# Attention in an MLP kernel: one float32 product, a reciprocal root from the table, later stages, batches hosted elsewhere

## The chip, the core and the metric

The kernel runs on one core of a Trainium2 chip. The metric is the device time of one execution in microseconds (us). The engines are named as the profile names them: PE is TensorE (PEld its weight loads), DVE is VectorE, ACT is ScalarE, POOL is GpSimd, SP is SyncE, which only issues DMAs here.

## The reference

Linear attention on 8 batches of 8 heads, 576 rows and 64 columns, then a normalisation by the root of the mean square, then two MLPs (512 to 2048 to 512) on the 4608 rows:

```python
kv  = np.einsum('bhsd,bhse->bhde', k, v)
out = np.einsum('bhsd,bhde->bhse', q, kv)
rms = np.sqrt(np.mean(out * out, axis=-1, keepdims=True) + 1e-06)
x   = out / rms * g_norm                      # then (b, s, h*e): 4608 x 512

h = x @ w_in                                  # first MLP
g = np.where(h >= 1, h, np.where(h <= -1, 0.0, (h + 1) ** 2 / 4))
x = g @ w_out
h = x @ w_in2                                 # second MLP
x = np.maximum(h, 0) ** 2 @ w_out2
```

## The kernel before

**Products.** The large products are made of three passes in a reduced-precision float32 format: an operand is split into a high part (a CAST on ACT, line 221) and the rest (a subtraction on DVE), and `mm3` (line 242) sums high by high, low by high and high by low. A tile of 128 x 512 in this format is one matmul.

**Order of the MLP work.** Five plain blocks come first: block b is the first MLP of batch b, 32 slots of 12 matmuls of 128x512 (4 output tiles of `ph` or 4 accumulators `acc`, three passes each). In a block, `u` is the activation's chain from `ph` (ACT lines 704 and 228, DVE line 706), and `gs` its split, which the `acc` matmuls read. Then six pairs of batches go through products with fewer multiplications (sums of blocks of the matrices, as in Strassen's method): `in_phase` makes `ph` at line 880, `out_phase` makes `po` at line 880, 336 matmuls each. The first two pairs are the second MLP of batches 0 to 3, the next two the first MLP of batches 5 and 6 with 7, and what follows is the second MLP of the rest.

**Attention.** It comes in pieces of two heads, (b, hp), four for each batch. `load_kv`, `load_q` fetch k, v, q through SP's queue. `kv_stage` makes `pkv` = k'v on PE (line 486) and copies its two diagonal blocks into `kvbd` as a high part (ACT, line 221) and a low part (DVE, line 499). `t_stage` transposes q on DVE and splits it (ACT line 221, DVE line 567). `o_stage` makes half of `po` by `mm3`, and from it two squares on ACT (lines 588, 589) and a scaled copy `o`. `r_stage` splits the squares (line 594), sums them over a head on PE (`pr`, line 608: against a matrix of ones, high part and rest), takes ln on ACT (line 609), then exp(-x/2) (line 611) to get a first root `y`, then a square and a Newton step on DVE (lines 526, 622, 623), and hands the result to the MLP as `x` or to DRAM. Two pieces, those in `WHOLE`, have an unsplit float32 product instead (line 576), and batch 0, at the very start, has its own functions (`t_first`, `o_first`, `r_first`). `pkv`, the attention's `po` and `pr` share a pool of two PSUM buffers; `kvbd` has two buffers.

**Where it stands.** `attention(base, every, order)` gives each step a slot. Batches 1 to 4 run in block b - 1, seven slots apart. `HOSTED` places the rest in the first two pairs: six pieces in pair 0 (batch 5, and two of batch 6) and six in pair 1, six slots apart. Block 4 hosts no attention.

**Weight sums.** The pairs need sums of blocks of the weights. They are made during blocks 1 to 4 in 16 units (`units`), 4, 4, 3 and 5 in a block: two loads of 512 KB by SP, some twenty operations of DVE (two are narrowing passes of two operations, two joins, eight sums, six splits), eight of ACT, and six stores of 512 KB that ACT's queue issues. Every engine takes its instructions in the order in which they were written down, so a step that waits holds up what stands behind it on its engine.

Of the kernel before, what the change touches and what calls it, by code (L numbers as in the profile page):

```python
# [10 lines left out]
F32 = mybir.dt.float32  # L11
# [5 lines left out]

LN_SCALE = 2.0**-44  # L20
# [57 lines left out]
def linear_attention_rms_two_mlps(  # L78
# [57 lines left out]
        0: ((5, 0), (5, 1), (5, 2), (5, 3), (6, 0), (6, 2)),  # L136
        1: ((6, 1), (6, 3), (7, 0), (7, 1), (7, 2), (7, 3)),
# [56 lines left out]
    lnb = const.tile([P, 1], F32, name="lnb")  # L194
    expb = const.tile([P, 1], F32, name="expb")
# [3 lines left out]
    kvbd = [const.tile([P, 2, P], F32R, name=f"kvbd{i}") for i in range(2)]  # L199
# [274 lines left out]
    def kv_stage(*pairs):  # L474
# [12 lines left out]
        for n, (b, hp) in enumerate(pairs):  # L487
            for j in range(2):
# [45 lines left out]
    def r_first(hp):  # L534
# [3 lines left out]
        for half in range(2):  # L538
# [3 lines left out]
            nc.scalar.activation(y[:, half], m, AF.Ln, bias=lnb, scale=LN_SCALE)  # L542
# [13 lines left out]
    def t_stage(b, hp):  # L556
        work = [ap1.tile([P, S], F32, tag=f"wk{n}", name=f"wk{n}_{b}_{hp}") for n in range(2)]
        if (b, hp) in WHOLE:
            qT = ap1.tile([P, S], F32, tag="hl0", name=f"qT_{b}_{hp}")
            nc.vector.transpose(qT, qs.pop((b, hp)))  # L560
            hl[b, hp] = (work, qT)
            return
# [33 lines left out]
    def r_stage(b, hp):  # L596
# [18 lines left out]
        for c, m in ms:  # L615
            newton(t[:, c], m)
# [35 lines left out]
    def attention(base, every, order):  # L652

        slots = []
        for j, (b, hp) in enumerate(order):
# [15 lines left out]
            if j == 0 and b < PLAIN:  # L671
                slots.append((s + 6, begin, b))
# [657 lines left out]
```

## Time and profile before

| | |
|---|---|
| device time, median of 3 runs | 1578.36 us (1578.21 to 1580.17) |
| the profiled execution's own time | 1577.18 us |
| its span | 1575.4 us |
| PE busy | 1544.0 us, 98% |
| DVE busy | 1195.8 us, 76% |
| ACT busy | 929.3 us, 59% |
| DMA, mean | 246 GB/s |

The profile is of one execution. A row of a timeline gives a start, a length and in brackets how long the engine had stood still before it and what ended that wait; matmuls overlap, so a row of several matmuls ends with the tail of the last one, and the distance between starts is shorter than a single length. A granted clock of 1.00 is 2.4 GHz; the lower of the two levels is 1.2 GHz.

### The profile page before, as it was taken

Reading aid. Unit: us, or ns where it says so; the run is one execution under the profiler, and the core shown is the slowest. Engines: PE = TensorE matmul, PEld = TensorE weight load, DVE = VectorE, ACT = ScalarE, POOL = GpSimd, SP = SyncE. Lnnn points to the kernel's source line nnn. Section 1 sums busy time; section 2 is a strip of 40 time slices with the busy share of each in tenths; the row PEclk is TensorE's granted clock in tenths of the full one; section 3 lists DMA queues with packets and bytes.
Section 4 is the critical chain, followed back from the end, with each engine's and each line's share of the span. In section 5 each row is a group of like instructions: output and inputs, shape, how many; then the busy total and the mean of one; then the engine's idle time right before and its main releaser. Section 6 shows DMA issues by size and latency. Waiting matters only on the chain.

```text
span 1575.4 us, 22379 instructions
## 1 busy us (share of the span) xinstructions
PE 1544.0 (98%) x7633; PEld 1268.9 (81%) x7633; DVE 1195.8 (76%) x2112; ACT 929.3 (59%) x1751; POOL 13.4 (1%) x30
## 2 busy tenths in 40 slices
PE   9999989999999999999989999999999999999999
PEld 5787768878877788787778888888888888888899
DVE  6975878786989678975689788868974597559666
ACT  5976666766756566735576466546653464446354
POOL 0000000000000000000000000000000000000000
PEclk9999999999999999999999999999999999999999
DMA  9676899796899966878767877776776676977797
GB/s 286 199 246 193 286 307 327 229 292 208 256 353 346 320 195 207 261 219 226 229 199 234 226 242 242 225 220 196 243 232 208 198 243 199 243 236 221 224 387 254
DMA packets 330914, 388.17 MB, mean 246 GB/s; under 512 B 197808, under 2 KB 223408, under 8 KB 330800
## 3 DMA queue, kind: packets, MB, share of 16 engines
q1 hardware_dynamic: 299904, 330.63, 69.2%
q10 hardware_dynamic: 30896, 56.11, 9.5%
q8 instruction: 61, 1.00, 0.3%
q14 instruction: 53, 0.43, 0.1%
HBM read 300.42 MB, written 86.25 MB: 245 GB/s over the span
## 4 chain that ended last, share of the span: by engine, by line
PE 84%; DVE 6%; ACT 5%; DMA 3%; issue 1%; SPq 0%; ACTq 0%; DVEq 0%
PE ph L880 32%; PE po L880 29%; PE acc L242 10%; PE ph L242 9%; PE pkv L486 1%; PE po L242 1%; PE pr L608 1%; DMA wsd<-s 1%; DVE s L189 1%; DVE u L706 1%; PE pwarm L1183 1%; DMA ws<-wsd 1%; DMA rest<-in_v_dram 0%; DVE t L809 0%; DMA wt<-wsd 0%
## 5 line engine op out<-in xcount | busy, mean ns | idle before, releaser
L880 PE MATMUL ph<-x,ws 128*128 128x512 f32 (+1 forms) x2352 | 507.1, 376 | 0.5 <-DVE e L936 0.5
L880 PEld LDWEIGHTS ph<-x,ws 128*128 128x128 f32 x2352 | 419.4, 189 | 79.5 <-DVE e L936 1.2
L880 PE MATMUL po<-t,ws 128*128 128x512 f32 x2016 | 461.7, 390 | 1.5 <-DMA ws<-wsd 0.8
L880 PEld LDWEIGHTS po<-t,ws 128*128 128x128 f32 x2016 | 377.1, 188 | 82.0 <-DVE t L809 3.3
L809 DVE TENSOR_TENSOR t<-g,t 128x512 fp32r<-128x512 f32 (+1 forms) x336 | 215.6, 647 | 84.1 <-ACT t L221 81.7
L221 ACT CAST t<-g 128x512 fp32r<-128x512 f32 (+1 forms) x336 | 195.5, 591 | 120.7 <-PE po L880 62.9
L242 PE MATMUL ph<-x,w 128*128 128x512 f32 x960 | 243.1, 396 | 7.6 <-DVE u L706 6.0
L242 PEld LDWEIGHTS ph<-x,w 128*128 128x128 f32 x960 | 177.4, 189 | 50.5 <-DVE u L706 10.5
L242 PE MATMUL acc<-gs,w 128*128 128x512 f32 x528 | 134.4, 398 | 3.5 <-DVE u L706 1.5
L957 ACT ACTIVATE g<-h 128x512 f32<-128x512 f32 (+1 forms) x120 | 70.4, 589 | 95.8 <-DVE h L946 95.8
L242 PEld LDWEIGHTS acc<-gs,w 128*128 128x128 f32 x528 | 98.6, 190 | 25.6 <-DVE u L706 2.0
L946 DVE CUSTOM_DVE_ANT_0 h<-ph,e 128x512 f32<-128x512 f32 (+1 forms) x120 | 76.1, 636 | 51.6 <-PE ph L880 47.6
L936 DVE TENSOR_TENSOR e<-ph,e 128x512 f32<-128x512 f32 (+1 forms) x112 | 72.1, 649 | 56.2 <-PE ph L880 47.8
L242 PE MATMUL acc<-gs,wt 128*128 128x512 f32 x432 | 106.5, 394 | 1.9 <-DVE gs L234 1.9
L242 PEld LDWEIGHTS acc<-gs,wt 128*128 128x128 f32 x432 | 81.8, 190 | 19.2 <-DVE gs L234 2.4
L221 ACT CAST x<-xr 128x512 fp32r<-128x512 f32 (+1 forms) x98 | 57.1, 590 | 41.7 <-DVE xr L860 23.5
L221 ACT CAST gs<-u 128x512 fp32r<-128x512 f32 x80 | 49.7, 622 | 47.4 <-DVE u L706 39.1
L706 DVE SCALAR_TENSOR_TENSOR u<-u,ph 128x512 f32<-128x512 f32 x80 | 54.4, 680 | 30.0 <-ACT u L228 29.9
L704 ACT ACTIVATE u<-ph,halfb 128x512 f32<-128x512 f32 x80 | 55.3, 691 | 24.7 <-PE ph L242 18.8
L234 DVE TENSOR_TENSOR gs<-u,gs 128x512 fp32r<-128x512 f32 x80 | 54.8, 686 | 17.1 <-ACT gs L221 16.6
L933 ACT COPY e<-ph 128x512 f32<-128x512 f32 (+1 forms) x56 | 30.8, 553 | 58.4 <-PE ph L880 51.5
L809 DVE TENSOR_TENSOR x<-xr,x 128x512 fp32r<-128x512 f32 (+1 forms) x98 | 62.6, 644 | 2.0 <-ACT x L221 1.9
(135 smaller groups left out, 1620.9 us busy)
## 6 DMA issues: line engine op xcount, KB each, us to landing
ws<-wsd SPq DMA_DIRECT2D x392, 512.0 KB, 4.4
wsd<-s ACTq DMA_DIRECT2D x96, 512.0 KB, 5.7
wt<-wsd SPq DMA_DIRECT2D x36, 512.0 KB, 5.5
raw<-in_moe_w_in_dram SPq DMA_DIRECT2D x32, 512.0 KB, 7.0
raw<-in_moe_w_out_dram SPq DMA_DIRECT2D x32, 512.0 KB, 6.1
xr<-x1d SPq DMA_DIRECT2D x36, 256.0 KB, 5.2
out_dram<-ov SPq DMA_DIRECT2D x142, 64.0 KB, 3.7
wsd<-w SPq DMA_DIRECT2D x17, 512.0 KB, 4.0
```

What stands on the lines that cost most here:

```text
L189: lo.tensor_tensor(t[:, :, 1, :], src, t[:, :, 0, :].bitcast(F32), ALU.subtract)
L221: return e.copy(dst, src)
L234: lo = engine(op + "_lo", phase).tensor_tensor(t[:, 1, :], src, t[:, 0, :].bitcast(F32), ALU.subtract)
L242: nc.tensor.matmul(dst, wt(a), xt(c), start=first and n == 0, stop=last and n == 2)
L704: nc.scalar.activation(u, ps, AF.Relu, bias=halfb, scale=0.5)
L706: nc.vector.scalar_tensor_tensor(u, u, 1.0, ps, op0=ALU.min, op1=ALU.max)
L809: engine2(op + "_lo").tensor_tensor(t[:, 1, :], src, t[:, 0, :].bitcast(F32), ALU.subtract)
L880: nc.tensor.matmul(ps, wt(a), xt(c), start=first and n == 0 and i == 0, stop=last and n == len(lhs) - 1 and i == 2, skip_group_check=True,)
L933: nc.scalar.copy(e[i, 1], bank)
L936: nc.vector.tensor_tensor(e[i, p], bank, e[i, 1], ALU.add)
L946: nc.vector._custom_dve(TENSOR_ADD_SAT, out=h, in0=bank, in1=add, s0=float("inf"), s1=0.0)
L957: nc.scalar.activation(g, h, AF.Square)
```

## The change

1. All pieces use an unsplit float32 product of q and kv, with one float32 `kvbd`. The split of q, the low part of `kvbd` and `mm3` there are gone.
2. The root comes from the table of ACT (`Abs_reciprocal_sqrt`) in place of ln and exp; o times y is formed before the Newton step, which leaves one operation behind it in place of two.
3. `o_stage` goes from slots s + 3, s + 4 to s + 4, s + 5, `r_stage` from s + 6 to s + 8, and pieces stand 6.7 slots apart in blocks (7 before) and 7 in pairs (6 before).
4. Batch 5 is hosted in block 4, batch 6 in pair 0, batch 7 in pair 1.
5. The weight-sum units are dealt 4, 5, 5, 2 to blocks 1 to 4 (an entry of `units` gives the kind, the number, the slot in the block, and now the delay of the join); the last ones of blocks 1, 2 and 3 start at slots 26, 28 and 30 of 32, where they stood at 29, 30 and 24.

```diff
     HOSTED = {
-        0: ((5, 0), (5, 1), (5, 2), (5, 3), (6, 0), (6, 2)),
-        1: ((6, 1), (6, 3), (7, 0), (7, 1), (7, 2), (7, 3)),
+        0: tuple((6, hp) for hp in range(NP)),
+        1: tuple((7, hp) for hp in range(NP)),
     }
...
-                t = kvbd[turn[b, hp] % len(kvbd)]
-                copy(engine("kv_hi", b), t[s, 0, s], ps[s, d])
-                nc.vector.tensor_tensor(t[s, 1, s], ps[s, d], t[s, 0, s].bitcast(F32), ALU.subtract)
+                copy(engine("kv_hi", b), kvbd[turn[b, hp] % len(kvbd)][s, s], ps[s, d])
...
-    def norm(t, y, o):
-        nc.vector.scalar_tensor_tensor(t, t, -3.0, y, op0=ALU.add, op1=ALU.mult)
-        nc.vector.tensor_tensor(t, o, t, ALU.mult)
+    def norm(dst, t, o):
+        nc.vector.scalar_tensor_tensor(dst, t, -3.0, o, op0=ALU.add, op1=ALU.mult)
...
-        qT = ap1.tile([P, S], F32, tag="wk2", name=f"qf_{b}_{hp}")
-        parts = [ap1.tile([P, S], F32R, tag=f"hl{n}", name=f"qT{n}_{b}_{hp}") for n in range(2)]
+        qT = ap1.tile([P, S], F32, tag="hl0", name=f"qT_{b}_{hp}")
         nc.vector.transpose(qT, qs.pop((b, hp)))
-        copy(engine("q_hi", b), parts[0], qT)
-        engine("q_lo", b).tensor_tensor(parts[1], qT, parts[0].bitcast(F32), ALU.subtract)
-        hl[b, hp] = (work, parts)
+        hl[b, hp] = (work, qT)
...
+        ps = bank(b, f"po_{b}_{hp}_{half}")
+        nc.tensor.matmul(ps[:, :U], kv, qT[:, c], start=True, stop=True)
...
-        mm3(ps[:, :U], lambda a: kv[:, a, :], lambda a: parts[a][:, c], True, True)
...
-            nc.scalar.activation(y[:, c], m, AF.Ln, bias=lnb, scale=LN_SCALE)
+            nc.scalar.activation(y[:, c], m, AF.Abs_reciprocal_sqrt, bias=epsb)
             ms.append((c, m))
-        nc.scalar.activation(y, y, AF.Exp, bias=expb, scale=-0.5)
...
         square(engine("y", b), t, y)
+        nc.vector.tensor_tensor(o, o, y, ALU.mult)
         for c, m in ms:
             newton(t[:, c], m)
         if b < PLAIN:
-            norm(t, y, o)
+            norm(t, t, o)
...
-        nc.vector.scalar_tensor_tensor(t, t, -3.0, y, op0=ALU.add, op1=ALU.mult)
-        nc.vector.tensor_tensor(o, o, t, ALU.mult)
+        norm(o, t, o)
...
-                (s + 3, o_stage, b, hp, 0),
-                (s + 4, o_stage, b, hp, 1),
+                (s + 4, o_stage, b, hp, 0),
+                (s + 5, o_stage, b, hp, 1),
             ]
+            late = 8
...
-            slots.append((s + 6, r_stage, b, hp))
+            slots.append((s + late, r_stage, b, hp))
         if b < PLAIN:
-            slots.append((2 * NF * b, store_xrem, b))
+            slots.append((2 * NF * b + 2, store_xrem, b))
...
-    for b in range(1, PLAIN):
-        jobs += attention(2 * NF * (b - 1), 7, [(b, hp) for hp in range(NP)])
+    for b in range(1, PLAIN + 1):
+        jobs += attention(2 * NF * (b - 1), 6.7, [(b, hp) for hp in range(NP)])
...
-        ((0, 4, 6), (1, 2, 16), (1, 6, 24)),
+        ((0, 5, 2, 4), (0, 6, 8, 6), (1, 2, 16, 5), (1, 6, 23, 5), (0, 7, 30, 6)),
...
-        for s, *job in sorted(attention(1, 6, HOSTED[n]), key=lambda j: j[0]):
+        for s, *job in sorted(attention(1, 7, HOSTED[n]), key=lambda j: j[0]):
...
-    nc.scalar.preload_act_table_set("natural_log_exp_and_others")
+    nc.scalar.preload_act_table_set("abs_reciprocal_sqrt_and_small")
```

Counted in the two programs, the attention's split products go from 156 matmuls of 128x288 to 52 float32 products, which the profile records as two matmuls each; ACT loses 26 casts of q, 28 passes of exp over 576 columns in the pieces and 4 in batch 0; DVE loses 26 subtractions for q and 52 of 64x64 for `kvbd`. The numbers of DMAs and of activations with a table function over 288 columns stay (64), and each program has one load of an activation table.

On PE in the second pair, near its start, where `pr` is the head sum, `po_6_1_1` (batch, piece, half) a half of the attention's product, and `ph1` an MLP matmul; before:

```order
L242 MATMUL po_6_1_1_7327<-qT1_6_1_7225,kvbd0_131 128x288
L242 MATMUL po_6_1_1_7327<-qT0_6_1_7224,kvbd0_131 128x288
L608 MATMUL pr_6_1_0_7406<-s2_6_1_7299,ones_123 128x288
L608 MATMUL pr_6_1_1_7410<-s2_6_1_7299,ones_123 128x288
L608 MATMUL pr_6_1_0_7406<-s2lo_6_1_7334,ones_123 128x288
L608 MATMUL pr_6_1_1_7410<-s2lo_6_1_7334,ones_123 128x288
L880 MATMUL ph1_6_0_7175<-x2_1_4_0_6748,ws2_0_0_4_7173 128x512 x3
L880 MATMUL ph1_6_0_7175<-x2_1_4_1_6948,ws2_0_0_4_7173 128x512 x3
L880 MATMUL ph1_6_1_7184<-x2_1_4_0_6748,ws2_0_0_4_7173 128x512 x3
L880 MATMUL ph1_6_1_7184<-x2_1_4_1_6948,ws2_0_0_4_7173 128x512 x3
L242 MATMUL po_6_3_0_7504<-qT0_6_3_7426,kvbd1_132 128x288
```

and now:

```order
L858 MATMUL ph1_6_1_7066<-x2_1_4_0_6635,ws2_0_0_4_7055 128x512 x3
L858 MATMUL ph1_6_1_7066<-x2_1_4_1_6835,ws2_0_0_4_7055 128x512 x3
L557 MATMUL po_7_0_1_7235<-qT_7_0_7101,kvbd0_130 128x288
L586 MATMUL pr_7_0_0_7324<-s2_7_0_7200,ones_123 128x288
L586 MATMUL pr_7_0_1_7328<-s2_7_0_7200,ones_123 128x288
L586 MATMUL pr_7_0_0_7324<-s2lo_7_0_7240,ones_123 128x288
L586 MATMUL pr_7_0_1_7328<-s2lo_7_0_7240,ones_123 128x288
L557 MATMUL po_7_1_0_7415<-qT_7_1_7292,kvbd1_131 128x288
L557 MATMUL po_7_1_1_7441<-qT_7_1_7292,kvbd1_131 128x288
L858 MATMUL ph1_5_0_7158<-x2_1_3_0_6610,ws2_0_0_3_7114 128x512 x3
```

The head sum of a piece still follows its product with no MLP matmul between; two new float32 products of the next piece now stand right behind it, ahead of the MLP matmuls.

On ACT in block 1 about `u1_1_10`, the eleventh tile of the activation chain (L704 and L228 before, L682 and L220 now, are its two activations; `s2_...` are casts of a weight-sum unit and the DMA rows its stores, which wait for splits that DVE makes); before:

```order
L704 ACTIVATE u1_1_9_2125<-ph1_1_9_2112,halfb_127 128x512
L181 DMA wsd2_1_0_118<-s2_1_0_3_2068 128x2x512
L221 CAST x1_2_1_1703<-t_2_1_1966 128x512
L228 ACTIVATE u1_1_9_2125<-u1_1_9_2125 128x512
L704 ACTIVATE u1_1_10_2174<-ph1_1_10_2161,halfb_127 128x512
L228 ACTIVATE u1_1_10_2174<-u1_1_10_2174 128x512
L221 CAST gs1_1_9_2143<-u1_1_9_2125 128x512
L221 CAST qT0_2_2_2002<-qf_2_2_2001 128x576
L221 CAST gs1_1_10_2202<-u1_1_10_2174 128x512
```

and now:

```order
L213 CAST s2_1_0_0_1963<-d2_1_0_1884 128x2x256
L682 ACTIVATE u1_1_10_2113<-ph1_1_10_2100,halfb_126 128x512
L587 ACTIVATE wk0_2_2_1902<-pr_2_2_0_2146,epsb_125 128x288
L213 CAST s2_1_0_1_1984<-d2_1_8_1914 128x2x256
L174 DMA wsd2_1_0_118<-s2_1_0_0_1963 128x2x512
L213 CAST s2_1_0_2_1987<-s12_2_1_0_1957 128x2x256
L213 CAST s2_1_0_3_2008<-s34_2_1_0_1958 128x2x256
L174 DMA wsd2_1_0_118<-s2_1_0_1_1984 128x2x512
L174 DMA wsd2_1_0_118<-s2_1_0_2_1987 128x2x512
L174 DMA wsd2_1_0_118<-s2_1_0_3_2008 128x2x512
L220 ACTIVATE u1_1_10_2113<-u1_1_10_2113 128x512
```

The two activations of `u1_1_10` stood next to each other; now a head's root, three casts of a weight-sum unit and its four stores stand between them.

## Rows read from the trace of the kernel before

**Rows 1.** The page: span, and busy time and instructions of TensorE.

```profile
span 1575.4 us, 22379 instructions
...
PE 1544.0 (98%) x7633; PEld 1268.9 (81%) x7633; DVE 1195.8 (76%) x2112; ACT 929.3 (59%) x1751; POOL 13.4 (1%) x30
```

**Rows 2.** Table of stretches: window, length, busy by engine, granted clock, DMA share, GB/s.

```profile
128.00:235.00 107.00, 100.31 (x522) 79.38 (x521) 75.34 (x142) 67.69 (x133) 4.04 (x4) 0.97 0.87 274
235.00:334.00 99.00, 99.00 (x520) 81.87 (x518) 81.61 (x156) 69.00 (x138) 2.06 (x5) 1.00 0.89 281
334.00:431.00 97.00, 95.81 (x480) 78.20 (x477) 78.20 (x148) 67.66 (x137) 1.55 (x4) 1.00 0.78 245
431.00:524.00 93.00, 91.75 (x429) 73.53 (x428) 81.25 (x155) 59.77 (x107) 0.41 (x1) 1.00 1.01 348
524.00:619.00 95.00, 92.58 (x479) 75.60 (x479) 65.97 (x114) 54.40 (x113) 0.00 (x0) 0.98 0.74 229
...
700.00:801.00 101.00, 91.48 (x497) 74.52 (x496) 61.41 (x106) 52.40 (x108) 0.00 (x0) 0.97 0.75 206
```

**Rows 3.** The chain that ended last, from 881 us: start, length, what.

```profile
881.59 76.16 PE ph L880 x336
...
1415.00 76.16 PE po L880 x336
```

**Rows 4.** Waits of TensorE: waited for, us in total, times, longest.

```profile
PE ph L242 <- DVE u L706: 6.0, 7, 2.5
...
PE pr L608 <- DVE kvbd L499: 3.5, 1, 3.5
```

**Rows 5.** Groups by line and shape: busy us, mean ns; then idle before.

```profile
L242 PE MATMUL po<-qT,kvbd 128*128 128x288 f32 x156 | 29.8, 304 | 5.3 <-ACT qT L221 4.1 <-DVE qT L567 1.1
...
L611 ACT ACTIVATE wk<-wk,expb 128x576 f32<-128x576 f32 x28 | 22.0, 784 | 0.3
...
L567 DVE TENSOR_TENSOR qT<-qf,qT 128x576 fp32r<-128x576 f32 x26 | 19.6, 753 | 5.8 <-ACT qT L221 5.5
...
L576 PE MATMUL po<-qT,kvw 128*128 128x288 f32 x8 | 2.3, 411 | 0.0
```

**Rows 6.** TensorE in order of time, block 0; columns: start, length, work [idle before].

```profile
65.17 1.13 PE L576 MATMUL po<-qT,kvw 128*128 128x288 f32 x4
```

**Rows 7.** The same view, second pair, three places.

```profile
714.70 0.96 PE L242 MATMUL po<-qT,kvbd 128*128 128x288 f32 x6
716.96 0.40 PE L608 MATMUL pr<-s,ones 128*128 128x288 f32 x1 [1.31 <-ACT wk L213]
717.96 0.40 PE L608 MATMUL pr<-s,ones 128*128 128x288 f32 x1 [0.59 <-ACT wk L213]
...
718.73 4.50 PE L880 MATMUL ph<-x,ws 128*128 128x512 f32 x12
...
751.80 0.67 PE L242 MATMUL po<-qT,kvbd 128*128 128x288 f32 x2 [3.89 <-ACT qT L221]
```

**Rows 8.** The same view, block 1 and the end of block 4.

```profile
176.06 4.59 PE L242 MATMUL acc<-gs,w 128*128 128x512 f32 x12 [1.49 <-ACT gs L221]
...
229.49 4.55 PE L242 MATMUL ph<-x,w 128*128 128x512 f32 x12 [2.50 <-DVE u L706]
...
527.26 3.10 PE L242 MATMUL acc<-gs,wt 128*128 128x512 f32 x7 [1.93 <-DVE gs L234]
```

**Rows 9.** Groups by line and shape: pieces of the chain behind a product.

```profile
L609 ACT ACTIVATE wk<-pr,lnb 128x288 f32<-128x288 f32 x56 | 26.8, 504 | 15.7 <-PE pr L608 15.5
L526 DVE SCALAR_TENSOR_TENSOR t<-pr,t 128x288 f32<-128x288 f32 x64 | 26.6, 450 | 3.4 <-ACT t L228 3.2
...
L594 DVE TENSOR_TENSOR s2lo<-wk,s 128x576 fp32r<-128x576 f32 x26 | 19.6, 755 | 15.3 <-ACT wk L589 15.1
```

**Rows 10.** Groups by line and shape: pieces of a weight-sum unit.

```profile
L189 DVE TENSOR_TENSOR s<-s,s 128x512 fp32r<-128x512 f32 x64 | 43.5, 683 | 8.3 <-ACT s L221 8.2
...
L365 DVE TENSOR_TENSOR s<-s,d 128x256 f32<-128x256 f32 x16 | 6.7, 417 | 0.0
```

More of the change, by code (lines that the diff above doesn't have):

```diff
@@ L193, in linear_attention_rms_two_mlps @@
     gvec = const.tile([P, 1], F32, name="gvec")
-    lnb = const.tile([P, 1], F32, name="lnb")
-    expb = const.tile([P, 1], F32, name="expb")
+    epsb = const.tile([P, 1], F32, name="epsb")
     halfb = const.tile([P, 1], F32, name="halfb")
@@ L198, in linear_attention_rms_two_mlps @@
     rests = [const.tile([P, 2, 2, D], F32, name=f"rest{i}") for i in range(2)]
-    kvbd = [const.tile([P, 2, P], F32R, name=f"kvbd{i}") for i in range(2)]
+    kvbd = [const.tile([P, P], F32, name=f"kvbd{i}") for i in range(2)]
     engines = {"A": nc.scalar, "D": nc.vector, "P": nc.gpsimd}
@@ L541, in r_first @@
             nc.tensor.matmul(m, ones.bitcast(F32), y[:, half], start=True, stop=True)
-            nc.scalar.activation(y[:, half], m, AF.Ln, bias=lnb, scale=LN_SCALE)
+            nc.scalar.activation(y[:, half], m, AF.Abs_reciprocal_sqrt, bias=epsb)
             ms.append(m)
-        nc.scalar.activation(y, y, AF.Exp, bias=expb, scale=-0.5)
         square(engine("y", 0), t, y)
+        nc.vector.tensor_tensor(o, o, y, ALU.mult)
         for half in range(2):
             newton(t[:, half], ms[half])
-        norm(t, y, o)
+        norm(t, t, o)
         n = TB // 2
@@ L557, in t_stage @@
         work = [ap1.tile([P, S], F32, tag=f"wk{n}", name=f"wk{n}_{b}_{hp}") for n in range(2)]
[L558 to L562, printed above, removed]
-        qT = ap1.tile([P, S], F32, tag="wk2", name=f"qf_{b}_{hp}")
-        parts = [ap1.tile([P, S], F32R, tag=f"hl{n}", name=f"qT{n}_{b}_{hp}") for n in range(2)]
+        qT = ap1.tile([P, S], F32, tag="hl0", name=f"qT_{b}_{hp}")
         nc.vector.transpose(qT, qs.pop((b, hp)))
-        copy(engine("q_hi", b), parts[0], qT)
-        engine("q_lo", b).tensor_tensor(parts[1], qT, parts[0].bitcast(F32), ALU.subtract)
-        hl[b, hp] = (work, parts)
+        hl[b, hp] = (work, qT)
     def o_stage(b, hp, half):
-        work, parts = hl[b, hp]
-        kv = kvbd[turn[b, hp] % len(kvbd)]
+        work, qT = hl[b, hp]
+        whole = (b, hp) in WHOLE
+        kv = kvw[:, hp % 2, :] if whole else kvbd[turn[b, hp] % len(kvbd)]
         c = slice(half * U, (half + 1) * U)
-        if (b, hp) in WHOLE:
-            ps = bank(b, f"po_{b}_{hp}_{half}")
-            nc.tensor.matmul(
-                ps[:, :U], kvw[:, hp % 2, :], parts[:, c], start=True, stop=True
-            )
+        ps = bank(b, f"po_{b}_{hp}_{half}")
+        nc.tensor.matmul(ps[:, :U], kv, qT[:, c], start=True, stop=True)
+        if whole:
             nc.scalar.activation(work[0][:, c], ps[:, :U], AF.Square)
@@ L585, in o_stage @@
         s2 = og[b, hp]
-        ps = bank(b, f"po_{b}_{hp}_{half}")
-        mm3(ps[:, :U], lambda a: kv[:, a, :], lambda a: parts[a][:, c], True, True)
         nc.scalar.activation(s2[0][:, c], ps[:, :U], AF.Square)
@@ L614, in r_stage @@
         square(engine("y", b), t, y)
+        nc.vector.tensor_tensor(o, o, y, ALU.mult)
         for c, m in ms:
@@ L617, in r_stage @@
         if b < PLAIN:
-            norm(t, y, o)
+            norm(t, t, o)
             nc.gpsimd.tensor_copy(xrem[b][:, hp, :], t[:, TB:])
@@ L1134, in linear_attention_rms_two_mlps @@
     for which, i, s0, j in [
-        (which, i, 2 * NF * (n + 1) + s, 4 if s in (0, 6, 12) else 6)
+        (which, i, 2 * NF * (n + 1) + s, j)
         for n in range(PLAIN - 1)
-        for which, i, s in units[n]
+        for which, i, s, j in units[n]
     ]:
```

14 lines of the change are left out of this document (5 added, 9 removed), and 6 rows, old and new, of the table units.

## The prediction

> **What bounds the kernel now.** The page comes first: TensorE is busy for 1544.0 of 1575.4 us [rows 1], so DVE at 76% and ACT at 59% have room on average, and work taken from them is worth nothing by itself. It pays only where TensorE stands still for it, or where an idle TensorE drops to its lower clock. The chain of waits then says where that cannot be: from 881 us on each phase of 336 matmuls of the pairs takes 76.16 us without a gap [rows 3], .227 us a matmul. Everything the change can win lies in the first 881 us. The table of stretches sizes it. A plain block has 32 x 12 matmuls, 87.0 us at .227; a phase of a pair has 76.2. Block 3 hosts four attention pieces in 97.0 us, so a piece costs TensorE at most 10.0/4 = 2.5 us. Against that measure block 1 (107.0) loses 10, block 2 (99.0) 2, block 4 (93.0, no piece) 6, pair 0 (95.0, six pieces) 3.8 and pair 1 (101.0, six) 9.8 [rows 2]: some 32 us. The waits of TensorE name the causes: the activation chain's DVE step `u`, and in pair 1 the split q (3.89 us once) and `kvbd` (3.5 once) [rows 4, 7]. A wait is paid twice: the granted clock is .97 in block 1 and in pair 1 [rows 2], and after waits of 1.49, 2.50 and 1.31 with .59 us twelve MLP matmuls took 4.59, 4.55 and 4.50 us [rows 7, 8], where 12 x .227 with a tail of .15 is 2.9. So each long wait costs 1.6 us more at 1.2 GHz.
>
> **The float32 product: +4.5 us.** This part lies on TensorE itself and nothing hides it. Six split matmuls last .96 us and one of them .304, so starts are (.96 - .304)/5 = .131 us apart [rows 5, 7]. The four float32 matmuls at 65.17 us (two products) last 1.13 and one of them .411: (1.13 - .411)/3 = .240 [rows 5, 6]. A piece had six of the one and gets four of the other: .960 - .786 = +.174, times 26 pieces = 4.5 us. The busy column would mislead: 29.8/156 x 6 = 1.15 us before and 2.3/8 x 4 = 1.15 after, equal, because busy time counts overlapping tails [rows 5]. Bounds: 4 to 5. The price by rows is 1.22 times the split product's. The Trainium skill ("FP8 and Floating Point Precision", TensorE Precision Notes) counts four passes for true float32 where the split makes three: by 4/3 the term would be 26 x .262 = 6.8 us. The measured row decides, and the sum keeps 4.5.
>
> **What DVE and ACT lose.** Per piece ACT drops the cast of q and the exp (.784), DVE the subtractions for q (.753) and `kvbd` [rows 5]; off the path this is free. On the path it shortens two chains: q no longer passes through ACT and back, and the root needs one ACT step less. At the start the last piece of batch 0 drops one exp and one operation after the Newton step, about 1.5 us; loads fill part of that, so I take **-1** (0 to -1.5). The table root has no row of before: I bound it by the ln of the same shape (.504) and the .784 of a 576-wide pass [rows 5, 9] and take the first, being the same 288 columns from PSUM with the same kind of bias; at the second, 56 x .28 = 16 us would land on an ACT that has hundreds to spare, and only the one tight chain below would show it (+.6).
>
> **Block 0: +1** (0 to 2). Products and head sums of batch 1 now meet at three places with no matmul between; each waits some tenths.
>
> **Block 1: -3.5** (-9 to +2). Its two large waits [rows 8], 1.49 + 1.7 and 2.50 + 1.7 = 7.4 us, hang on how steps meet on DVE and ACT, and the order has changed there. But a new place comes. On ACT three casts and four stores of a weight-sum unit now stand between the two activations of `u1_1_10`, and on DVE 17 operations stand between `u1_1_9` and `u1_1_10`. By the rows of their kinds (seven 256-wide or like them at .417, eight 512-wide at .683, two 576-wide at .755 [rows 9, 10]) they take 9.9 us. The step itself (.7) and the two activations ahead of `u1_1_9` (about 2) come on top; TensorE has 24 MLP matmuls (5.4), one float32 pair of products (.96) and the head sums (.5) to go on with, 6.9. That leaves a wait of about 12 - 7 = 5, with the clock 6.6; in its bounds 2 (rows overlap where DVE is full) to 7. What it replaces is 10.
>
> **Blocks 2 and 3: +1.5** (-2 to +18, see the rivals). They are dealt one and two weight-sum units more; since a block's last unit runs on into the next block (blocks 1 and 2 end with one at slots 29 and 30 of 32 before, blocks 1, 2 and 3 at 26, 28 and 30 now), each really gets about one more. A unit is about 20 DVE operations, half of .417 and half of .683 [rows 10], 11.0 us; the lighter pieces give back at least four times .753 [rows 5] in each block. DVE would be busy for about 81.6 + 11 - 3 = 90 of 99 us and 78.2 + 11 - 3 = 86 of 97, some nine tenths; block 4 stood at 81 of 93 [rows 2] and lost 6. Against that, pieces and head sums now stand two slots or more apart in the order of these blocks, 5.4 us of cover. I take the low value because block 2 before, at 82 of 99, lost 2 only.
>
> **Block 4 and pair 0: -5** (-9 to -1). Block 4 gives up three units (33 us of DVE; their loads and 18 stores of 512 KB, where DMA was full at 1.01 and 348 GB/s [rows 2]) and takes in four pieces. The wait at its end, 1.93 us with slow matmuls behind it (seven in 3.10 where 1.75 is normal), 3.3 in all [rows 8], should go, and about half of its many short waits for `u`. Loads of v in block 4 now stand on SP's queue behind steps of the second MLP's input; what is queued there is due later, so I cost it at nothing, up to +2.
>
> **Pair 1: -4** (-10 to +1). Counted from start to start, it loses at 714.70 to 718.73 (ten matmuls of .131 in 4.03 us) 2.7 and 1.6 for the clock; at 751.80 3.9 and about 2.4 in slow matmuls; for `kvbd` 3.5 and some tenths: 15 us [rows 4, 7]. Six pieces become four, so q is not late three times. But TensorE's order still has a product, its head sum and the next piece's products in a row. The chain there: two squares on ACT (.8), the split (.755), the sums (.3), two roots (.9), a square (.78), o times y (.755), two Newton steps (.9) [rows 5, 9], about 5.2 us, with 1.0 of TensorE's own work in it: 4.2, and 1.6 for the clock. Two later places: head sums behind four copies of `kvbd` on ACT (1.4), and `po_7_2`, whose transposed q stands on DVE behind eight operations (5.1 us) with only 12 matmuls (2.7) as cover: 2.4 and 1.6. Sum 11.2, so about 4 less than 15.
>
> **The sum.** -1 + 1 - 3.5 + 1.5 - 5 - 4 + 4.5 = -6.5 us against the profiled execution's 1577.18: 1570.7. The median of the runs is 1.2 above that execution, so about 1572.
>
> **Rivals.** (a) *The waits go altogether.* If block 1, block 4, pair 0 and pair 1 lose no more than block 3 does, some 30 us go, 4.5 come: 1577.2 - 30 + 4.5 - 1 = 1551, 1552 as a median. For it: block 3 shows that four pieces and three units fit with next to no wait [rows 2], and chains are shorter everywhere. Against it: the two spots above stand in the built order.
> (b) *Slower: DVE in blocks 2 and 3.* With five units and four pieces each, more than block 1 had (four and four, 10 lost [rows 2]), a block could lose as much as that one: its `u` steps queue behind a unit's operations and TensorE follows. Ten each instead of the 2 and 0 of before are +18 in place of +1.5, so 16.5 on the forecast: 1587 for the profiled execution, 1588 as a median. It decides the sign from about 10 us above the forecast. Against it: block 2 had four units and lost 2.
> (c) *No change.* The new places of block 1 and pair 1 cost what the old ones did (+7.5 on the forecast): 1578 for the profiled execution, 1579 as a median. For it: both are priced by chains that rows only bound.
> (d) *The root costs a table change each time.* ACT's stream in the changed program holds one table load, as before, so this has no chance. By itself: the Trainium skill ("ScalarE: Activation LUTs", What ACT_TABLE_LOAD costs) gives 1283 ns for a load, and no run here shows a second one.
>
> **How the numbers follow.** About .2% (3.2 us) is what a measurement of this kernel can tell from no change. Forecast, 1566 to 1578: .42, of which .06 lies above 1575.2; (a), and what lies between it and the forecast: .22; (c): .16; (b): .18; .02 for something slower that I do not see. Faster: .36 + .22 + .02 of (c) = .60; same: .06 + .14 = .20; slower: .20. The range goes from 1555, near (a), to 1585, short of (b)'s full price; about .08 is left out below and .1 above.
>
> **What would show it.** Each step has its mark in the profile of the changed kernel: phases from the third pair on still at 76.16 us; four float32 matmuls of a piece about .24 apart; `u` rows in block 1 with one wait of about 5 us at the eleventh tile; block 4 under 97 us with four pieces and DMA well under 348 GB/s; pair 1 with a wait of 4 behind the first head sum. Stretches of blocks 2 and 3 above 102 us each would make (b) right; a pair 1 of 86 to 88 us and a block 1 of 98 us would make (a) right; float32 matmuls more than .26 apart would break the first term.

## The result: slower, 1590.5 us

The changed kernel takes 1590.5 us (median of 4 runs, 1589.9 to 1590.7) where the kernel before took 1578.5 beside it: 1.0077 of it, 95% interval 1.0065 to 1.0088. The forecast was 1572 us and 1555 to 1585; rival (b), at 1588 us, is nearest: its time and its place came true, its cause only in part, as the runs below show.

The page of the changed kernel, to be held against [rows 1]:

```profile
span 1588.1 us, 22122 instructions
...
PE 1548.1 (97%) x7581; PEld 1270.0 (80%) x7581; DVE 1169.7 (74%) x2033; ACT 895.9 (56%) x1693; POOL 10.0 (1%) x30
```

TensorE is busy for 4.1 us more, and the span has grown by 12.7; so it stands still longer, though DVE and ACT have less to do than before (74% and 56%). Where, the lengths of the blocks tell. They are worked out from the start of the first MLP matmul of each in the trace, in us; "in" and "out" are the two phases of a pair:

| | start | bl. 0 | 1 | 2 | 3 | 4 | pair 0 in | out | pair 1 in | out |
|---|---|---|---|---|---|---|---|---|---|---|
| before | 27.4 | 100.4 | 107.2 | 99.4 | 97.0 | 92.1 | 95.9 | 80.1 | 101.6 | 80.3 |
| changed | 29.6 | 100.5 | 107.9 | 109.5 | 104.3 | 96.8 | 92.8 | 77.0 | 97.5 | 77.8 |

From pair 2 on both take 694 us, as the chain said [rows 3]. Blocks 2 and 3 have grown by 10.1 and 7.3 us, 17.4 together. Block 4 (4.7 longer, with four pieces more) and the two pairs have together shrunk by 8.1, and the start is 2.2 later. The table of stretches, cut at the changed kernel's own blocks (block 1 to pair 0's first phase, and pair 1's; columns as in [rows 2]):

```profile
130.10:238.10 108.00, 98.87 (x486) 78.25 (x484) 71.33 (x129) 63.00 (x126) 0.78 (x3) 0.97 0.88 272
238.10:347.60 109.50, 102.56 (x509) 82.90 (x510) 86.02 (x162) 68.28 (x138) 2.09 (x4) 0.98 0.98 300
347.60:451.90 104.30, 99.31 (x498) 80.43 (x497) 85.10 (x161) 66.06 (x134) 1.75 (x4) 0.98 0.87 279
451.90:548.70 96.80, 96.80 (x497) 79.47 (x496) 76.64 (x137) 66.52 (x135) 0.64 (x1) 1.00 0.89 280
548.70:641.50 92.80, 90.76 (x469) 74.17 (x467) 55.36 (x90) 46.86 (x95) 0.00 (x0) 1.00 0.72 221
718.50:816.00 97.50, 89.24 (x446) 72.14 (x444) 53.70 (x85) 44.82 (x90) 0.00 (x0) 0.96 0.76 204
```

Blocks 2 and 3 show it: DVE is busy for 86.0 of 109.5 and 85.1 of 104.3 us, less than the nine tenths I had feared, and still TensorE has 7 and 5 us of idle time and a clock below 1.00 in them. So DVE is not full; something comes in the wrong order or late. The waits of TensorE (us in total, times, longest), against [rows 4]:

```profile
PE ph L234 <- DVE u L684: 15.5, 8, 5.7
PE po L557 <- DVE qT L548: 3.8, 1, 3.8
PE po L557 <- DVE t L516: 2.1, 1, 2.1
```

The wait for `u` has gone from 6.0 to 15.5 us; those for the split q are gone and that for `kvbd` is down from 3.5 to .8, but two for the transposed q and for the Newton step have come in their place. The long ones, TensorE in order of time, first in blocks 1 and 2, then in pair 1:

```profile
202.50 0.80 PE L234 MATMUL ph<-x,w 128*128 128x512 f32 x1 [5.73 <-DVE u L684]
...
278.49 4.60 PE L234 MATMUL ph<-x,w 128*128 128x512 f32 x12 [3.51 <-DVE u L684]
```

```profile
736.89 0.65 PE L557 MATMUL po<-qT,kvbd 128*128 128x288 f32 x2
...
739.25 0.40 PE L586 MATMUL pr<-s,ones 128*128 128x288 f32 x1 [1.58 <-ACT wk L205]
...
742.24 1.43 PE L557 MATMUL po<-qT,kvbd 128*128 128x288 f32 x4 [2.06 <-DVE t L516]
743.10 3.13 PE L858 MATMUL ph<-x,ws 128*128 128x512 f32 x6
...
776.53 1.58 PE L557 MATMUL po<-qT,kvbd 128*128 128x288 f32 x4 [3.77 <-DVE qT L548]
777.50 4.86 PE L858 MATMUL ph<-x,ws 128*128 128x512 f32 x13
```

The wait of 5.73 us is the one for the eleventh `u` of block 1, priced at 5. In pair 1 stand the two places that the order had shown: behind the first head sum 1.58 and 2.06, then six matmuls in 3.13 us; and 3.77 for `po_7_2`, with thirteen in 4.86. The first was priced right too (4.2 with 1.6), the second lower (2.4 with 1.6).

The chain of waits between 238 and 285 us tells who is late in block 2 (start, length, what):

```profile
271.08 5.33 DMA wsd<-s
...
276.49 0.63 ACT s L213
...
277.14 0.57 DVE s L182
...
277.75 0.69 DVE u L684
...
278.46 0.38 ACT gs L213
```

A store of a weight-sum unit (`wsd<-s`) is on its way for 5.33 us. A cast `s` on ACT waits for it, since its buffer is the one that this store reads; DVE's half of the same split (`s`, L182) waits for the cast, and `u` stands behind it on DVE. So `u` at 277.75 and TensorE at 278.49 are late. ACT's waits of this kind (us in total, times, longest), before and changed:

```profile
ACT s L221 <- DMA wsd<-s: 4.6, 3, 2.1
```

```profile
ACT s L213 <- DMA wsd<-s: 25.8, 9, 4.5
```

### The profile page after: what moved, and what is told of

Read it like the earlier page. It is cut to its first block, busy times and chain, and to the rows that moved or that the text cites. A ratio compares the mean times of both kernels' runs of the same rounds, so it can differ in the third digit from the quotient of the medians.

```text
span 1588.1 us, 22122 instructions
## 1 busy us (share of the span) xinstructions
PE 1548.1 (97%) x7581; PEld 1270.0 (80%) x7581; DVE 1169.7 (74%) x2033; ACT 895.9 (56%) x1693; POOL 10.0 (1%) x30
## 4 chain that ended last, share of the span: by engine, by line
PE 85%; DMA 7%; DVE 4%; ACT 3%; issue 1%; SPq 0%; ACTq 0%; DVEq 0%
PE ph L858 31%; PE po L858 30%; PE acc L234 10%; PE ph L234 10%; DMA wsd<-s 3%; PE po L557 1%; PE pkv L478 1%; DMA raw<-in_moe_w_in_dram 1%; DMA wt<-wsd 1%; PE pr L586 1%; DVE d L267 1%; DMA v<-in_v_dram 0%; DVE t L787 0%; DVE w L182 0%; DVE t L516 0%
## 5 line engine op out<-in xcount | busy, mean ns | idle before, releaser
L234 PE MATMUL ph<-x,w 128*128 128x512 f32 x960 | 245.7, 401 | 16.5 <-DVE u L684 15.5
L234 PE MATMUL acc<-gs,wt 128*128 128x512 f32 x432 | 109.9, 401 | 2.4 <-DMA wt<-wsd 1.4
L682 ACT ACTIVATE u<-ph,halfb 128x512 f32<-128x512 f32 x80 | 55.2, 690 | 22.2 <-PE ph L234 15.7
```

Of the source, the lines that this page charges most:

```text
L234: nc.tensor.matmul(dst, wt(a), xt(c), start=first and n == 0, stop=last and n == 2)
L682: nc.scalar.activation(u, ps, AF.Relu, bias=halfb, scale=0.5)
```

## Experiments: the weight-sum units

Each run's time stands beside the kernel before on the same chip (1578.0 to 1579.4 us), with the ratio and its 95% interval in brackets. Block lengths are of one profiled execution of each run.

**units_back** undoes the dealing in the changed kernel:

```diff
...
-        ((0, 2, 0, 4), (0, 3, 6, 6), (1, 1, 14, 5), (1, 5, 21, 5), (0, 4, 28, 4)),
...
+        ((0, 2, 5), (1, 1, 14), (1, 5, 22), (0, 3, 30)),
...
```

> The changed kernel with one part undone: the weight-sum units dealt 4, 4, 3, 5 to blocks 1 to 4 with their old slots and joins. In the changed kernel block 2 lasts 109.5 us and block 3 104.3, against 99.3 and 97.1 before. Theory U (the fifth units in blocks 2 and 3 make the activation chain late): blocks 2 and 3 fall to about 101 and 99 us, block 1 loses its 5.7 us wait at the eleventh tile, block 4 rises from 96.8 to 102 or more, and the whole is 1578 to 1584 us. Theory P (the pieces' new places and later stages make it late): blocks 2 and 3 stay above 104 and 101, and the whole is 1588 us or more.

1585.2 us (ratio 1.0035, 1.0022 to 1.0049). Blocks 1 to 3 last 105.4, 101.0 and 97.6 us, as theory U says, and theory P falls: the dealing is worth 15.2 of the 17.4 us. One mark of U failed: the wait of 5.7 us in block 1 is still there. But block 4, now with five units and four pieces, takes 109.0, and so only 5 of the 17 us come back in the sum.

**units_alone** deals 4, 5, 5, 2 in the kernel before.

> The kernel before with one part of the change: units dealt 4, 5, 5, 2, all else as before, so that block 4 has two units and no attention piece. Theory U: blocks 2 and 3 rise by 5 to 10 us each, block 4 falls by 4, pair 0 by 2: 1583 to 1590 us. Theory P: blocks 2 and 3 stay within 2 us of 99 and 97, block 4 gains: 1572 to 1578 us.

1598.6 us (1.0131, 1.0116 to 1.0146): 20 us slower by a table alone. Blocks 1 to 3 take 113.8, 107.3 and 106.0, block 4 gains only 3.3. With the heavier pieces of before the units cost even more in blocks 1 to 3 (23.5 us; 17.7 in the changed kernel, held against units_back), more than either theory had.

**units_even** deals 4, 4, 4, 4 in the changed kernel.

> The changed kernel with units dealt 4, 4, 4, 4, eight slots apart in blocks 1 to 3 (seven in block 4). With five units a block with four pieces lost about 14 us (blocks 2, 3 and, with the old dealing, 4), with four 4 to 6, with two none. Theory U in either form: block 2 about 101, block 3 about 101 (one unit more than the 97.6 of the old dealing), block 4 about 101: 1578 to 1583 us, under both the changed kernel (1590.5) and the old dealing (1585). If what counts is where a unit's steps meet the pieces and not how many there are: 1585 or more.

1584.0 us (1.0030, 1.0019 to 1.0042). Blocks 1 to 3 as expected (106.2, 100.5, 98.7); block 4 not: 109.0 with four units, as with five. **mix1** (below) has 107.2 with three, in an execution 4 us above the median of its run, against 96.8 with two. In block 4 of units_even TensorE waits once for long, for a split behind `u`:

```profile
PE acc L234 <- DVE gs L226: 3.9, 1, 3.9
```

So by these profiles four pieces and three units are too much for block 4, though block 3 carries them in 97 us before. What differs is that batch 5's pieces go to DRAM (`xrd<-wk`, for which ACT waits 4.3 us in this block of units_even and 7.1 in that of mix1) and that the pairs' first inputs are made in this block; which of them it is was not tried.

**ring4_b4.** The units' splits share four buffers; at the start of block 4 four more are added. This run leaves these out in the kernel before, and changes nothing else:

```diff
-    hook(last + 1, prep_ring.add, *((xp, f"x{KD + i}") for i in range(KD)))
```

> The kernel before, but the four extra buffers that the units' split tiles get at the start of block 4 are left out, so that block 4's five units share four buffers as the units of blocks 1 to 3 do; nothing else changes. Moving units to blocks 2 and 3 alone has cost 20 us, far more than DVE time can say. Theory R (the four shared buffers: a cast on ACT waits until the store of the split four earlier has landed, and the activation chain stands behind it): block 4 rises from 92.1 us to 97 to 104, ACT waits longer for stores, the whole is 1583 to 1591 us. Theory D (DVE's own load and its order): block 4 stays within 2 us, the whole is 1577 to 1581.

1587.2 us (1.0048, 1.0030 to 1.0065). Block 4 rises from 92.1 to 97.6 us, no other block by more than half a microsecond, and ACT's wait for stores from 4.6 to:

```profile
ACT s L221 <- DMA wsd<-s: 23.9, 15, 3.5
```

The profiled execution is the fastest of four; by the medians the run is 8.4 us slower, 3 more than this block explains. Still, the buffers do it: five units in a block of four buffers cost 5.5 us that they don't cost with eight. This is what moving units out of block 4 did: it took them from the block with eight buffers to blocks with four.

**owe1** hands a store to ACT's queue one slot after its split and not two, in the changed kernel, so that a buffer comes free 2.7 us sooner:

```diff
-            owe(2, dst, t[:, hs])
+            owe(1, dst, t[:, hs])
```

> The changed kernel with each store of a weight-sum split handed to ACT's queue one slot after its split was written down, not two, so that the four buffers come free a slot (2.7 us) sooner. Theory R: ACT waits less for stores (25.8 us before), blocks 2 and 3 gain 2 to 6 us together, 1584 to 1589. But a store that stands nearer to its split makes ACT wait for DVE: if that is the cause of the late activations, blocks 1 to 3 lose another 3 to 10 us, 1593 or more. Theory D: within 2 us of 1590.5.

1583.3 us (1.0030, 1.0017 to 1.0043): 7 of the 12 us are back. Blocks 2 and 3 take 103.9 and 98.5 us (109.5 and 104.3 before the edit), and ACT's wait is:

```profile
ACT s L213 <- DMA wsd<-s: 5.2, 4, 3.0
```

**units_alone_owe1** is the same edit on top of units_alone.

> The kernel before with units dealt 4, 5, 5, 2 (1598.6 us alone, 20 above before), and each store of a split handed over one slot sooner. If the four shared buffers carry all of the 20 us: 1578 to 1583. If they carry the share that the same edit gave back in the changed kernel (7 of 12 us): 1586 to 1592. If DVE's load carries it: 1596 or more.

1596.5 us (1.0114, 1.0096 to 1.0133): only 2 come back, less than the two intervals can tell apart, though ACT's wait is down to 3.7 us here too (14.5 without the edit). By what was expected this speaks for DVE. What remains stands on DVE and ACT in the order of their queues:

```profile
PE ph L242 <- DVE u L706: 11.2, 7, 3.5
PE po L242 <- ACT qT L221: 5.8, 6, 3.9
```

Taken together: the earlier store gives back most of the loss of blocks 2 and 3 in the changed kernel (11.4 of 17.4 us by the block lengths), where pieces are light and late; with the heavy pieces of before 5.7 of 16.9. That this is the buffers is shown directly for block 4 alone (ring4_b4); for blocks 2 and 3 it rests on ACT's waits for stores, which fell with the loss, and no run gave these blocks more buffers. The rest shows as waits for `u` and for the split q with ACT's wait for stores gone, so probably in the work and the order of DVE's and ACT's queues; no run took the units' work itself away.

**stores_pool** lets POOL issue the stores, so that they hold up nothing on ACT.

> The changed kernel, but the units' stores (and the stores of the first MLP's result) are issued by POOL in place of ACT, in the same order, so that a store that waits for a split on DVE holds nothing up on ACT. If the waits of blocks 1 to 3 come from ACT standing behind such stores: the 5.7 us wait at the eleventh tile of block 1 falls under 2, blocks 2 and 3 lose 3 to 8 us each, the whole is 1572 to 1582 us. If they come from the four buffers that the units' splits share, or from DVE's own load: block 1 gains, blocks 2 and 3 stay within 3 us, the whole is 1584 to 1590 us. If the issue on POOL is itself slow: above 1592 us.

1599.8 us, 9 slower than the change. The wait at the eleventh tile goes (no wait for `u` is above 2.4 us), but the store itself takes longer, 6.8 us to land in block 2 where 5.0 is the median from ACT's queue, POOL needs .7 us to issue one and waits for splits and sums in its turn, and ACT's 25 us of waiting for buffers stay. Blocks 2 and 3 gain nothing (109.0 and 105.5), and the 9 us are lost in blocks 1 and 4 (110.9 and 106.5), where waits of TensorE for a load of weights (7.6) and for a Newton step (5.9) have come. A queue of its own doesn't help when the buffers are what is short.

## Experiments: the product and the root

The four runs below leave slots, hosting and units as before.

**root_product** has both, **product_alone** the float32 product, **root_alone** the root with the change's order behind it.

> The kernel before with the float32 product and the table root, and nothing of the schedule: slots, hosting and units as before. Both theories: TensorE pays 4.5 us for the product, and the shorter chains give back some 3 to 8 of the waits in pair 1 and block 1: 1573 to 1581 us. A third theory (the product and the root themselves shift the engines' order and cost the 12 us): 1586 us or more, with the start later by 2 us as in the changed kernel.

> The kernel before with the float32 product alone (ln and exp kept, slots, hosting and units as before). By the rows TensorE pays 26 x .174 = 4.5 us; what comes back can only be the waits for the split q and for kvbd (3.9 and 3.5 us in pair 1, .8 in block 1). If those go: 1575 to 1580. If another step is late in their place, as the runs with root and product hint: 1580 to 1584.

> The kernel before with the table root alone. Root and product together gave 1582 us (1576.6 to 1583.7), some 3 above before, with 4.5 us priced for the product on TensorE. If the product costs what its rows say and the root gives 0 to 2: 1575 to 1579 us here. If the root itself costs (its new order of steps makes the start later, by 1 to 2 us): 1579 to 1582.

In this order 1582.4 us (1.0018, 1.0004 to 1.0032), 1577.3 (.9991, .9981 to 1.0001) and 1581.8 (1.0021, 1.0009 to 1.0032). So the product costs nothing in the sum, though TensorE pays for it. The changed kernel's rows, the group and two in order of time:

```profile
L557 PE MATMUL po<-qT,kvbd 128*128 128x288 f32 x104 | 33.1, 414 | 5.9 <-DVE qT L548 3.8 <-DVE t L516 2.1
...
L587 ACT ACTIVATE wk<-pr,epsb 128x288 f32<-128x288 f32 x56 | 27.0, 500 | 2.6 <-PE pr L586 2.2
```

```profile
362.70 0.65 PE L557 MATMUL po<-qT,kvbd 128*128 128x288 f32 x2
362.97 1.08 PE L234 MATMUL acc<-gs,w 128*128 128x512 f32 x3
```

Two float32 matmuls last .65 us and one .414, so they start .24 apart: the term of 4.5 us stands, and with the product alone about as much comes back: blocks 1 and 3 and pair 0 are .7 to 1.4 shorter with it inside, block 2 and pair 1 1.5 and 2.2 longer. The root's activation takes 500 ns, as the ln did (504, [rows 9]). And yet the root costs 3 us.

**root_old_norm** keeps the root and undoes the order behind it (against root_alone; the removed line at the end stood ahead of the Newton step):

```diff
-        nc.vector.scalar_tensor_tensor(dst, t, -3.0, o, op0=ALU.add, op1=ALU.mult)
+        nc.vector.scalar_tensor_tensor(t, t, -3.0, y, op0=ALU.add, op1=ALU.mult)
+        nc.vector.tensor_tensor(t, o, t, ALU.mult)
...
-        nc.vector.tensor_tensor(o, o, y, ALU.mult)
...
```

> The kernel before with the table root but the old order behind the Newton step (two operations of 576 columns after it, none ahead). If the operation that the change puts ahead of the Newton step (o times y, .75 us on DVE while the head sum's buffer is held) makes the start and pair 1 later: 1577 to 1580 us, and the clock from 14 to 28 us is 1.00. If it is the root itself or the chance of the start: 1580 to 1584.

1577.9 us (.9994, .9984 to 1.0003; ten runs, 1575.1 to 1580.1, against ten of root_alone, 1578.2 to 1586.1). So in the kernel before it is the order, worth some 4 us. By what way is less clear. In the change o times y (.75 us on DVE) stands ahead of the two Newton steps. At the start of the changed kernel the warm-up matmuls wait for such a step:

```profile
21.86 0.81 PE L1161 MATMUL pwarm<-warm 128*128 128x512 bf16 x3 [1.17 <-DVE t L516]
```

and the stretch from 14 to 28 us of before, root_alone and root_old_norm (length, then busy by engine, clock, DMA share) shows the clock:

```profile
14.00:28.00 14.00, 12.56 (x87) 7.10 (x86) 12.04 (x27) 10.39 (x21) 0.87 (x2) 1.00 1.03 307
```

```profile
14.00:28.00 14.00, 12.79 (x83) 7.77 (x84) 11.82 (x26) 9.34 (x21) 0.47 (x2) 0.88 1.16 316
```

```profile
14.00:28.00 14.00, 12.47 (x87) 7.48 (x87) 11.85 (x28) 9.79 (x22) 0.87 (x2) 1.00 1.15 314
```

The clock is 1.00, .88 and 1.00. That looks like the order, but two other profiles speak against it. The same stretch of best2 (below), with the old order, and of units_even, with the new one:

```profile
14.00:28.00 14.00, 12.47 (x82) 7.43 (x81) 11.45 (x24) 9.51 (x21) 0.87 (x2) 0.88 1.13 303
```

```profile
14.00:28.00 14.00, 12.49 (x88) 7.66 (x89) 13.11 (x29) 9.25 (x20) 0.47 (x2) 1.00 1.15 314
```

Of nine profiles with the table root and the new order eight have .88 there, of two with the old order one, of nine with ln and exp none. So the lower clock comes with the root, mostly, and the order doesn't decide it. From the first head sum to the thirteenth MLP matmul it takes 21.6 us before; with the root 20.3 (old order) and 20.6 (new) where the clock stays at 1.00, and 21.6 to 22.2 with either order where TensorE falls to 1.2 GHz for a while. The shorter chain is worth a good 1 us there, and the lower clock takes it away. The second place is pair 1, 2.4 us longer in root_alone. TensorE in order of time, root_alone first:

```profile
753.52 2.12 PE L239 MATMUL po<-qT,kvbd 128*128 128x288 f32 x6 [3.18 <-ACT qT L218]
755.44 15.93 PE L875 MATMUL ph<-x,ws 128*128 128x512 f32 x60
...
794.77 0.61 PE L604 MATMUL pr<-s,ones 128*128 128x288 f32 x1 [3.46 <-DVE kvbd L496]
...
795.42 10.95 PE L875 MATMUL ph<-x,ws 128*128 128x512 f32 x36
```

```profile
750.30 0.53 PE L239 MATMUL po<-qT,kvbd 128*128 128x288 f32 x2 [3.18 <-ACT qT L218]
751.09 1.33 PE L239 MATMUL po<-qT,kvbd 128*128 128x288 f32 x4 [0.27 <-DVE qT L563]
752.22 14.84 PE L875 MATMUL ph<-x,ws 128*128 128x512 f32 x60
...
790.46 0.40 PE L604 MATMUL pr<-s,ones 128*128 128x288 f32 x1 [3.45 <-DVE kvbd L496]
...
790.83 9.97 PE L875 MATMUL ph<-x,ws 128*128 128x512 f32 x36
```

The waits are the same, 3.18 and 3.5 us, and so is the time of the six matmuls (2.12 us in both, from the first start to the last end). What stands behind is slower in root_alone: 60 MLP matmuls in 15.93 us instead of 14.84, 36 in 10.95 instead of 9.97, a head sum in .61 instead of .40. The granted clock of this phase is .93 in root_alone and .97 in root_old_norm, so it is the clock again, after equal waits. Why it fell further in one execution these rows don't show, and it isn't tied to the order: the changed kernel, with the new one, has .96 there and noroot, with the old, .95. So the 4 us are shown by ten runs of each, and how the order costs them stays open.

**noroot** is the changed kernel with ln, exp and the old order.

> The changed kernel with ln and exp in place of the table root, and the old order behind the Newton step; all else is the change. The root alone cost 3 us (1581.8 against 1578.8) where it takes work from ACT and DVE: a later start, at the lower clock (0.88 from 14 to 28 us), and 2.8 us in pair 1. If that cost is the root's: 1585 to 1589, start at 27.5 to 28.5 us. If it came only with the old schedule: 1589 to 1593; above that, the lighter chain was a help.

1589.3 us (1.0062, 1.0049 to 1.0075): 1 less than the change, which the intervals don't tell apart, with the start at 28.3 us. Against the 17 us of blocks 2 and 3 the root is the small part.

## Experiments: stages and hosting

**stages_back** puts the stages of the changed kernel back to s + 3, s + 4 and s + 6, pieces 7 apart in blocks.

> The changed kernel with the stages back at slots s + 3, s + 4 and s + 6 and pieces 7 apart in blocks (the two pairs keep 7 and their hosting; units 4, 5, 5, 2 stay). If the later stages give the pieces cover (as I had it in blocks 2 to 4): waits of TensorE for pr and po return, 1592 to 1600 us. If they cost, by meeting the units' steps: 1582 to 1588. If the four shared buffers are all there is: within 2 us of 1590.5, blocks 2 and 3 still above 104 and 101.

1596.8 us (1.0111, 1.0096 to 1.0126), 6 slower than the change: blocks 1, 3 and 4 are 1.7 to 2.9 longer (block 2 is 2.5 shorter), pair 1 takes 101.3 instead of 97.5. The later stages are a gain, and the change had hidden it.

**host_alone_owe1** is the schedule part of the change (hosting, stages, units) with the earlier store, with split product, ln and exp.

> The kernel before with the schedule part of the change (hosting, later stages, units 4, 5, 5, 2) but the split product and ln and exp kept, and each store of a split handed over one slot sooner. With that earlier store the changed kernel fell from 1590.5 to 1583.3 us. If product and root cost 3 to 5 us there too (4.5 on TensorE, some at the start): 1577 to 1581. If the lighter pieces are what lets block 4 host four of them: block 4 above 100 us, 1584 or more.

1586.9 us (1.0051, 1.0036 to 1.0066). Block 4 takes 97.6 with the heavy pieces as with the light ones, so that expectation falls; blocks 2 and 3 take 107.2 and 101.5 where owe1 had 103.9 and 98.5. The lighter pieces are worth 6 us there by these profiles; by the medians the two runs are 3.6 apart, and their intervals overlap.

**mix1** is the change with the earlier store and units 4, 4, 5, 3.

> The changed kernel with the earlier store and units dealt 4, 4, 5, 3. With four units and the earlier store block 2 should lose no more than block 3 with three (100 us after 103.9), block 3 stays at 98.5, block 4 with three units and four pieces lies between its 98.5 with two and 109 with four: 100 to 104. Whole: 1580 to 1585 us. Below 1578.8 it would beat both kernels.

1586.5 us (1.0052, 1.0034 to 1.0071), 3 more than owe1: block 4 takes 107.2, more than expected. It doesn't beat owe1, and neither beats the kernel before.

**product_late** takes only the float32 product and the later stages (with pieces 6.7 apart in blocks) into the kernel before:

```diff
-                (s + 3, o_stage, b, hp, 0),
-                (s + 4, o_stage, b, hp, 1),
+                (s + 4, o_stage, b, hp, 0),
+                (s + 5, o_stage, b, hp, 1),
...
-            slots.append((s + 6, r_stage, b, hp))
+            slots.append((s + 8, r_stage, b, hp))
```

> The kernel before with the float32 product and the change's later stages (s + 4, s + 5, s + 8, pieces 6.7 apart in blocks, six in pairs as before), and its own hosting, units, ln and exp. The product alone gave 1577.3 against 1578.0; taking the later stages out of the changed kernel cost 6 us. If later stages help wherever pieces meet the rest: 1570 to 1575, pair 1 under 100 us (103.8 with the product alone), faster than both kernels. If they only helped because units stood close in blocks 1 to 3: 1576 to 1580.

1571.1 us (.9950, .9936 to .9964): faster than both kernels. Pair 1, six pieces as before, takes 93.1 us (101.6 before, 103.8 with the product alone). The waits in its first 60 us, TensorE in order of time, against [rows 7]:

```profile
716.93 0.40 PE L595 MATMUL pr<-s,ones 128*128 128x288 f32 x1 [1.22 <-ACT wk L213]
717.92 0.59 PE L595 MATMUL pr<-s,ones 128*128 128x288 f32 x1 [0.59 <-ACT wk L213]
...
749.10 11.09 PE L867 MATMUL ph<-x,ws 128*128 128x512 f32 x47 [0.84 <-DMA ws<-wsd]
```

The head sum behind its first product still waits (1.22 and .59); the waits of 3.89 and 3.5 us are gone. The changed kernel needs 97.5 us for this phase with two pieces fewer; what of its hosting, its spacing and its root costs that, no run separates, and none tried the hosting alone.

**product_late_owe1** adds the earlier store, **best2** the root with its old order instead.

> The same with each store of a split handed over one slot sooner. With units dealt 4, 4, 3, 5 ACT waits only 4.6 us for the four buffers in the kernel before and 10.3 with the product alone, so there is little to win: within 2 us of the run without it. If the buffers matter here too: 2 to 5 us less.

> The float32 product, the later stages and the table root with the old order behind the Newton step; hosting and units as before. Product with later stages gave 1571.1 us. The root with the old order cost nothing alone (1577.9 against 1579.0). If the shorter ACT chain now helps pair 1 and block 1: 1567 to 1570. If it only shifts the start to a later phase: 1571 to 1574.

1571.7 us (.9952, .9939 to .9966) and 1574.3 (.9974, .9964 to .9985). With units 4, 4, 3, 5 the buffers are no bound, and the earlier store changes nothing. The root with the old order, free in the kernel before, makes this one 3 us slower (the intervals just touch), near what was expected if it only shifts the start: blocks 1 and 3 and pair 1 are 2.7, 2.0 and 1.2 us shorter than in product_late, block 2 and pair 0 2.6 and 2.0 longer, and the start came 4 later in that execution.

## Why the prediction was wrong

The forecasts below leave out the float32 product, priced by itself; the changed kernel's lengths hold it, .7 us where a block has four pieces.

- **The step that failed is blocks 2 and 3:** +1.5 us, measured +17.4, of which 15.2 go when the old dealing is put back (units_back). I had the right rival and its price (18), and the number of units (one more in each, 23 stores of splits became 29 and 28). I took the low value because block 2 had carried four units with a loss of 2, and priced a unit by DVE's time alone. What that price left out is the four buffers and the way of a store (two slots of delay and 5 us to land) before one is free: 11.4 us come back when the stores go a slot sooner. ACT's waits in the trace of before name it (4.6 us), and the argument had no row of them. The other 6 us stay open; a step of DVE or ACT that queues behind a unit's operations, as rival (b) had it, fits them, though DVE stayed at 79 and 82%, under nine tenths.
- **Start:** -1, measured +2.2. The saving was about right where the clock held: from the first product of k and v to the thirteenth MLP matmul it takes 28.0 us before and 27.4 in units_even, which has the same start. In this execution it takes 28.7: the clock fell behind a wait of 1.17 us in the chain (it did not in units_even, behind the same wait), and the term had neither. Another .66 of the 2.2 is the loads: that first product starts at 6.36 us in this execution and at 5.70 in that of before.
- **Block 1:** -3.5, measured +.7. The new wait was priced right (5, measured 5.73), and the two that were to go (1.49 and 2.50) are gone. But a wait for a load (1.44) and several short ones stand beside it, so that TensorE is idle for 9.1 us where it was for 6.7, the clock is .97 as before, and .7 us is the product. **Block 0:** +1, measured +.1.
- **Block 4 and pair 0:** -5. The three lengths shrink by 1.5 together, while 4 pieces came and 2 went, 4.4 us of TensorE's work at 2.2 each: 5.9 less lost. Right in sum.
- **Pair 1:** -4. Both phases shrink by 6.6 us, 4.4 of them the two pieces less, so 2.2 less lost where 4 was forecast. The two places of the order came as priced; the last one was longer (3.77 for 2.4).
- **The float32 product:** +4.5 on TensorE, right by its rows. That it is free in the sum was missed: I counted the relief of q and `kvbd` under pair 1 only.
- **Rivals:** (a) fell with blocks 2 and 3, and pair 1 (97.5 us, 86 to 88 wanted) shows it wrong too. (b) was right on the blocks and the price, and half right on the cause. (c) was right for block 1 and not for pair 1. (d) had no part.

## What to carry to other kernels

A step that is moved takes its buffers' limits with it: before pricing it by an engine's time, count the buffers that it shares at the new place and how long one is held (issue delay and landing of the store that reads it). What a shorter chain saves can be lost again when TensorE's clock falls behind a wait in it, as at the start here. And a bundle of edits can hide a gain: here product and later stages alone gave 8 us, and dealing, hosting and the root took 20.

## What the runs showed of the hardware

A float32 product of 128x288 shows as two matmuls whose starts lie .24 us apart. In the trace of before its busy time is that of three split ones (1.15 us a piece both ways [rows 5]), in the changed kernel 1.27 us a piece, and neither is the .174 us more that the starts give. Stores issued by POOL landed after 6.8 us in block 2 where those of ACT's queue took 5.0, with the same sizes (6.5 and 5.3 over the whole kernel). And the start varies by some microseconds: the first product started between 5.5 and 6.4 us in nine profiles of kernels with ln and exp and between 6.1 and 7.6 in eleven with the table root; with one profile of each kernel, chance and kernel can't be told apart.

```profile
L174 POOL DMA_DIRECT2D wsd<-s x96 | 68.9, 719 | 258.6 <-DVE s L182 72.8 <-DVE d L266 64.3 <-issue 23.7
```

Each issue occupied POOL for .72 us, 68.9 in all, and POOL stood still for 259 us ahead of them: in order, it waits for DVE as ACT did.
